# 214 added products of the identity ahead of 43 of TensorE's tasks in a state-space and FFN block

## The chip, the core and the metric

The kernel runs on one core of a Trainium2 chip. The metric is the time of one execution on the device, in microseconds (us); lower is better. A core has five engines that run side by side, each through its own queue, in the order written: TensorE (PE in the profile; its weight loads are PEld), VectorE (DVE), ScalarE (ACT), GpSimd (POOL) and SyncE (SP), which here issues nearly all DMA transfers. TensorE writes only to PSUM, eight banks of 128 partitions by 512 float32 each. The profile also tells the granted clock of TensorE, as a share of full speed.

## What is computed

The reference, cut to what matters. A layer norm modulated by a condition `c`, a long convolution (a diagonal state-space kernel, in the reference through an FFT of 4096 points), and a gated FFN behind a second modulated layer norm. L is 2048, D 640, N 128, FF 1728; all float32.

```python
def _A_ref(u, log_A_real, A_imag, C_real, C_imag, log_dt, D_skip):
    dt = jnp.exp(log_dt)
    A = -jnp.exp(log_A_real) + 1j * A_imag
    C = (C_real + 1j * C_imag) * dt[:, None]
    P = jnp.exp((A * dt[:, None])[:, :, None] * pos[None, None, :])
    K = 2.0 * jnp.einsum("dn,dnl->dl", C, P).real
    y = irfft(rfft(u_t, 2 * L) * rfft(K, 2 * L))[:, :, :L]
    return y + u * D_skip
def _B_ref(x, w1, w3, w2):
    return (_silu(x @ w1) * (x @ w3)) @ w2

sa, ca, ga, sb, cb, gb = split(_silu(c) @ w_mod, 6)
x = x + ga * _A_ref(_layernorm(x) * (1 + ca) + sa, ...)
x = x + gb * _B_ref(_layernorm(x) * (1 + cb) + sb, w1, w3, w2)
```

## The kernel before

**Stages.** The convolution is done in five blocks of 128 channels. For a block `b`, the generator builds the kernel K in eight chunks (tasks `g{b}.{c}`): GpSimd makes phases and magnitudes (`ph`, `z0` to `z2`), ScalarE sines (`s0` to `s4`), VectorE their products (`m0` to `m4`), and TensorE multiplies `xx` by `yy` into the tile `kps` (task `g{b}.{c}.p`, 64 matmul records each); ScalarE and VectorE then move `kps` into `ks` (`r` and `d`). The normed input of the block is made by tasks `h{b}.{i}` in tiles `hn`, `hb` and sent through HBM. A first transform of input and kernel follows (`hh{b}.{i}.m` and `k{b}.{i}.m`, tiles `ps`, 16 records each), copied to `sp` by ScalarE or VectorE (`.e`). The second transform is `w{b}.{i}.f` and `w{b}.{i}.k` (tiles `fh` and `fk`); ScalarE holds `fh` in `hz` (`.h`), VectorE multiplies (`.x0`, `.x1`, `.c`, into `fp`), and `z{b}.{j}.z` transforms back into two `fz` tiles, which go to HBM as `zt` (`v0`, `v1`, `o0`, `o1`).

**Before and behind these.** The condition's row is multiplied with `w_mod` (`mr0` to `mr4` and `mc0` to `mc4`, tile `pm`), the row is spread over the partitions (`pr0` to `pr3`, tile `prow`), and parameters are transposed (`q0.t*`, `q1.t*`, tile `ptp`). Behind block 4 come the last inverse step on the rows (`iy0` to `iy7`, then `iyb0` and `iyb1` on data read back from HBM as `izb`), the second layer norm, its transposes (`tp0.k`, `tp1.k`), and the first FFN products (`pp0.k`, `pp1.k`, tile `gu`; then `dn` into `acc`). After that a hand-ordered FFN runs (tiles `X`, `c`, `acc`), in which nothing is changed.

**Order.** Up to the first FFN products all work is a list of tasks in a planner (`Plan`). Each task has an engine, an assumed duration, predecessors, and the buffers it takes and gives. `Plan.place` puts them into one order by assumed times and ranks (`RANKS`); `Plan.run` then calls the tasks' functions in that order, and `InOrder` chains all instructions of an engine, so that no engine runs its instructions in another order than the plan's. The instructions pass through `InOrder`, so that their profile line is that one helper's (L157) whatever the task; groups are told apart by tile names.

**Banks.** `kps` is one bank, its halves used in turn by even and odd chunks (a chunk's product waits until `r` and `d` of the chunk two before it are done). The tiles with the tag `f` rotate through three banks and the tag `x` has one more; `pbank` deals these four out in turn. `tr` has three banks, which the sines use. A task's first instruction waits for its bank to be released by the readers of the tile before, and for its operands. At `border` these pools close and the FFN's open (five accumulators, `acc0` to `acc4`, and three `gu` banks); `tp*` are put into the accumulators' banks, `iyb*` into `gu`.

**A float32 product** shows in the trace as two matmul records, each with its weight load (32 products of `kps` are 64 records); a transpose is one record. The helper that makes a tile of transposes, as one example of such a task:

```python
def turn(self, ps, tag, bufs, src):
    n = src.shape[1]
    pt = ps.tile([P, 512], F32, name="ptp", tag=tag, bufs=bufs)
    for k in range(n):
        self.turned(pt[:, k * P:k * P + P], src[:, k, :])
```

Of the kernel before, what the change touches and what calls it, by code (L numbers as in the profile page):

```python
# [31 lines left out]
G0 = 17  # L32
SIGN = -2 ** 31
RANKS = """
# [133 lines left out]
class Plan:  # L168
# [101 lines left out]
    def run(self):  # L270

        T = self.tasks
        found = [int(x) for x in RANKS.split()]
        searched = [n for n in T if n not in self.own]
        assert len(found) == len(searched)
        self.order = self.place({n: t[4] for n, t in T.items()} | dict(zip(searched, found)))
        for s, f, e, n in self.order:
            if T[n][2]:
                T[n][2](e)


class K:
# [238 lines left out]
    def param_load(self, T, bs):  # L521
        for nm, src in (("cr", self.c_re), ("ci", self.c_im), ("ai", self.a_im)):
            self.nc.sync.dma_start(T[nm], src.rearrange("(k p) n -> p k n", p=P)[:, bs])

    def turn(self, ps, tag, bufs, src):
        n = src.shape[1]
        pt = ps.tile([P, 512], F32, name="ptp", tag=tag, bufs=bufs)
        for k in range(n):
            self.turned(pt[:, k * P:k * P + P], src[:, k, :])
        return pt[:, :n * P].rearrange("p (b c) -> p b c", b=n)  # L530
# [63 lines left out]
    def gen_chunk(self, d0, tabs, off, E, place):  # L594
# [37 lines left out]
        def product():  # L632
            kps = place()
            for e in range(C // 4):
                for q in range(4):
                    i = e * 4 + q
                    for r in range(2):
                        nc.tensor.matmul(kps[q * 32:(q + 1) * 32, e * 64:(e + 1) * 64], xx[:, r, i, :],
                                         yy[:, r, i, :, :].rearrange("p a b -> p (a b)"),
                                         start=(r == 0), stop=(r == 1), tile_position=(0, 32 * q))  # L640
# [432 lines left out]
    def tail_tasks(self, border, cut):  # L1073
# [109 lines left out]
        def rows(b, rank):  # L1183
            for j in range(4 * b, 4 * b + 4):
                u = j // 2

                def inv(j=j, u=u):
                    py = bank[j] = self.pbank(f"iy{j}")
                    for pr in range(2):
                        self.nc.tensor.matmul(py[pr * 64:pr * 64 + 64, :cut], self.wd[j // 4][:, j % 4, pr, :], z[u][pr][:, j % 2, :],  # L1190
                                              start=True, stop=True, tile_position=(0, pr * 64))
# [23 lines left out]
        def last_inv(b):  # L1215
            py = bank["b"] = self.bank(f"iyb{b}").rearrange("p (j d) -> p j d", j=4)
            for j in range(4):
                for pr in range(2):
                    self.nc.tensor.matmul(py[pr * 64:pr * 64 + 64, j], self.wd[b][:, j, pr, :], z["b", b][:, pr, j], start=True, stop=True, tile_position=(0, pr * 64))
# [16 lines left out]
        def prepare(b, rank):  # L1236
# [15 lines left out]
            for k in range(KT):  # L1252
                r = rank + .1 + .1 * k + b

                def tp(k=k):
                    bank["t", b, k] = self.acc_bank(f"tp{b}{k}", k)
                    self.channels(bank["t", b, k], [xn[b, j] for j in range(4)], k)

# [16 lines left out]
        def plain(b, tiles, p, rank, after):  # L1275
            banks = {}

            def mm(k):
                if k == 0:
                    for m in tiles:  # L1280
                        banks[m] = [self.bank(f"gu{b}{m}{i}") for i in range(2 if m < 13 else 1)]
                x = list(self.x_of(X, b, k))
                for m in tiles:
# [423 lines left out]
    def turn_steps(self, T, where, bs):  # L1707
# [8 lines left out]
        def turn(i):  # L1716
            k, o = (i, 0) if n > 1 else (0, i * P)
            if k not in x:
                x[k] = where()
            for b in range(n):  # L1720
                self.turned(x[k][:, o + b * P:o + b * P + P], T[("fi", "at", "ai", "mx")[i]][:, b, :])
            x["v", i] = x[k][:, o:o + n * P].rearrange("p (b c) -> p b c", b=n)
# [89 lines left out]
    def first_tasks(self, b, m):  # L1812
# [6 lines left out]
        def mm(i):  # L1819
            pk[i] = self.psg.tile([P, 512], F32, name=f"ps{b}{m}{i}", tag="f", bufs=3) if b == 0 else self.pbank(f"ps{b}{m}{i}")  # L1820
            for e in range(4):
                x = self.ks[b][:, 4 * i + e, :] if m else xb[:, :, 4 * i + e]
# [28 lines left out]
    def spectra_tasks(self, b):  # L1851
# [6 lines left out]
        def of(m, i):  # L1858
            ps = bank[m, i] = four(self.pbank(f"f{'hk'[m]}{b}{i}"))
            for q in range(2):  # L1860
# [25 lines left out]
        def inverse(j):  # L1886
            p = prod.pop(j).rearrange("p r q d -> p r (q d)")
            for f in range(2):
                bank["z", j, f] = self.pbank(f"fz{b}{j}{f}")
            for r in range(2):  # L1890
                for f in range(2):
# [108 lines left out]
    def early_tasks(self, e):  # L2000
# [76 lines left out]
        def row(k):  # L2077
            if k == 0:
                pm[0] = self.psx.tile([P, 512], F32, name="pm0", tag="x")
            self.mod_row(pm[0], k)  # L2080
        for k in range(KT):
# [17 lines left out]
        def spread(g):  # L2099
            pr[g] = ps.tile([P, 512], F32, name=f"prow{g}", tag="f", bufs=3)  # L2100
            n = 512 if g < 3 else 384
            nc.tensor.matmul(pr[g][:, :n], bc(self.ident[:, 32 * g], 1, P), mt[0][:, :n], start=True, stop=True)

# [22 lines left out]
        def col(k):  # L2126
            if k == 0:
                pm[1] = self.psx.tile([P, 512], F32, name="pm1", tag="x")
            self.mod_row(pm[1], k, w[k])
        for k in range(KT):  # L2130
# [45 lines left out]
```

## Time and profile before

| | |
|---|---|
| time of three runs, median (lowest to highest) | 970.81 us (970.12 to 972.39) |
| the profiled execution, time on the device | 972.31 us |
| the same execution, first to last instruction (span) | 970.5 us |
| PE, DVE, ACT, POOL busy, share of the span | 89%, 72%, 56%, 35% |
| mean granted clock of TensorE | 0.975 |
| DMA | 127.31 MB, mean 131 GB/s |

The span is 1.8 us shorter than the profiled execution's own time, which is at the upper end of the runs. Up to some 290 us VectorE is busy nine tenths of the time in most stretches and TensorE six to nine; from there on TensorE is busy nearly all the time, apart from a stretch around 380 us between the convolution and the FFN. A matmul record's end is modelled, so that records overlap; the distance from one start to the next is the better price of one. In the rows of the timeline the first number is the start, the second the length of a group of records, the bracket at the end the idle time ahead of it and what ended it.

### The profile page before, as it was taken

Reading aid. Unit: us, or ns where it says so; the run is one execution under the profiler, and the core shown is the slowest. Engines: PE = TensorE matmul, PEld = TensorE weight load, DVE = VectorE, ACT = ScalarE, POOL = GpSimd, SP = SyncE. Lnnn points to the kernel's source line nnn. Section 1 sums busy time; section 2 is a strip of 40 time slices with the busy share of each in tenths; the row PEclk is TensorE's granted clock in tenths of the full one; section 3 lists DMA queues with packets and bytes.
Section 4 is the critical chain, followed back from the end, with each engine's and each line's share of the span. In section 5 each row is a group of like instructions: output and inputs, shape, how many; then the busy total and the mean of one; then the engine's idle time right before and its main releaser. Section 6 shows DMA issues by size and latency. Waiting matters only on the chain.

```text
span 970.5 us, 20551 instructions
## 1 busy us (share of the span) xinstructions
PE 859.9 (89%) x7985; PEld 681.8 (70%) x7985; DVE 702.0 (72%) x1395; ACT 546.4 (56%) x1022; POOL 340.5 (35%) x371
## 2 busy tenths in 40 slices
PE   1464787889899997899999999999999999999997
PEld 1132665767778884677777778888788888888775
DVE  7998899999999968886767677557456464645422
ACT  6877788979888851564434455346444344443412
POOL 1797889879799600002111111000011212120000
PEclk9996999999999999799999999999999999999999
DMA  9955453723425268935434422276342322220374
GB/s 218 275 168 191 111 136 95 177 66 106 111 80 152 74 159 206 241 118 182 122 120 139 122 96 68 82 209 194 112 134 64 102 77 86 82 82 28 108 220 133
DMA packets 110506, 127.31 MB, mean 131 GB/s; under 512 B 10568, under 2 KB 90696, under 8 KB 109128
## 3 DMA queue, kind: packets, MB, share of 16 engines
q1 hardware_dynamic: 109032, 125.21, 45.3%
q8 instruction: 63, 1.03, 0.5%
q10 hardware_dynamic: 1376, 0.79, 0.3%
q14 instruction: 35, 0.29, 0.1%
HBM read 95.82 MB, written 30.15 MB: 130 GB/s over the span
## 4 chain that ended last, share of the span: by engine, by line
PE 70%; DVE 17%; ACT 5%; issue 4%; DMA 3%; POOL 1%; SPq 1%; ACTq 0%; DVEq 0%
PE c L157 19%; PE acc L157 18%; PE X L157 12%; PE ps L157 4%; PE gu L157 3%; DVE yy L157 3%; PE kps L157 3%; PE fz L157 2%; PE fk L157 2%; DVE fp L157 2%; PE fh L157 2%; DVE hn L157 2%; DVE xx L157 2%; DVE xb L157 1%; ACT tr L157 1%
## 5 line engine op out<-in xcount | busy, mean ns | idle before, releaser
L157 PE MATMUL acc<-ah,w 128*128 128x512 f32 x560 | 173.2, 395 | 2.4 <-DMA w<-w2d 1.7
L157 PEld LDWEIGHTS acc<-ah,w 128*128 128x128 f32 x560 | 103.7, 188 | 26.4 <-issue 2.1
L157 PE MATMUL acc<-al,w 128*128 128x512 f32 x260 | 102.4, 394 | 0.0
L665 DVE TENSOR_TENSOR wl<-s,wh 128x256 fp32r<-128x256 f32 x92 | 38.9, 423 | 67.5 <-ACT wh L664 67.1
L841 POOL TENSOR_TENSOR s<-wr 128x256 f32<-128x256 f32 x22 | 16.4, 744 | 187.8 <-DMA wr<-in_w 94.8
L157 POOL TENSOR_TENSOR ph<-p,p 128x1024 int32<-128x1024 int32 x40 | 79.2, 1979 | 8.2 <-ACT tr L157 8.0
L664 ACT ACTIVATE wh<-s 128x256 fp32r<-128x256 f32 x92 | 37.6, 410 | 78.5 <-PE X L157 58.1
L157 PE MATMUL kps<-yy,xx 128*32 128x64 f32 x2560 | 51.8, 234 | 28.6 <-DVE xx L157 21.4
L157 DVE TENSOR_TENSOR yy<-yy,tr 128x512 f32<-128x512 f32 (+1 forms) x80 | 75.3, 943 | 1.2 <-ACT tr L157 0.6
L157 PEld LDWEIGHTS kps<-yy,xx 128*32 128x32 f32 x2560 | 45.1, 116 | 38.3 <-issue 22.0
L664 ACT ACTIVATE wh<-wr 128x256 fp32r<-128x256 f32 x92 | 38.4, 418 | 56.0 <-PE X L157 42.3
L842 POOL TENSOR_TENSOR s<-s,wr 128x256 f32<-128x256 f32 x22 | 16.6, 755 | 134.0 <-issue 133.9
L902 ACT ACTIVATE t<-g 128x512 f32<-128x512 f32 x44 | 27.8, 632 | 52.7 <-DVE g L866 52.7
L157 ACT ACTIVATE tr<-ph,hpi 128x512 f32<-128x512 f32 x80 | 54.6, 690 | 4.4 <-DVE xx L157 2.7
L157 PEld LDWEIGHTS acc<-al,w 128*128 128x128 f32 x260 | 48.9, 188 | 10.8 <-DVE al L665 0.3
L871 DVE SCALAR_TENSOR_TENSOR g<-t,g 128x512 f32<-128x512 f32 x48 | 33.7, 702 | 31.3 <-ACT t L902 29.3
L157 POOL TENSOR_TENSOR yy<-e,e 128x512 f32<-128x512 f32 x48 | 52.4, 1109 | 8.8 <-PE kps L157 5.9
L157 DVE TENSOR_TENSOR xx<-tr,xx 128x512 f32<-128x512 f32 x80 | 54.3, 680 | 1.1 <-ACT tr L157 1.1
L157 PE MATMUL ps<-wk,ks 128*64 128x128 f32 x640 | 42.4, 285 | 13.6 <-DVE ks L157 8.9
L157 ACT ACTIVATE tr<-ph 128x512 f32<-128x512 int32 x80 | 47.3, 598 | 12.4 <-DVE yy L157 6.5
L157 PE MATMUL ps<-wk,xb 128*64 128x128 f32 x640 | 46.1, 295 | 6.3 <-ACT sp L157 3.0
L157 PEld LDWEIGHTS ps<-wk,ks 128*64 128x64 f32 x640 | 37.0, 143 | 20.3 <-ACT hn L157 6.6
(448 smaller groups left out, 2379.7 us busy)
## 6 DMA issues: line engine op xcount, KB each, us to landing
w<-w2d SPq DMA_DIRECT2D x42, 640.0 KB, 3.9
wr<-in_w SPq DMA_DIRECT2D x50, 320.0 KB, 3.9
zd<-zt SPq DMA_DIRECT2D x40, 256.0 KB, 2.9
w2d<-w SPq DMA_DIRECT2D x14, 640.0 KB, 3.5
xs<-in_x SPq DMA_DIRECT2D x16, 320.0 KB, 11.3
hs<-hb SPq DMA_DIRECT2D x20, 256.0 KB, 2.5
xb<-hs SPq DMA_DIRECT2D x20, 256.0 KB, 4.9
iz<-zd SPq DMA_DIRECT2D x32, 160.0 KB, 5.0
```

What stands on the lines that cost most here:

```text
L157: self.prev = self.k.order(f(*a, **kw), self.prev)
L664: self.nc.scalar.activation(H, v, AF.Copy)
L665: eng.tensor_tensor(Lo, v, H.bitcast(F32), op=ALU.subtract)
L841: eng.tensor_tensor(s[0], u[:, 0:2], u[:, 2:4], op=ALU.add)
L842: eng.tensor_tensor(s[1], s[0], g[:, 0:2], op=ALU.subtract)
L871: V.scalar_tensor_tensor(g, th, 1.0, g, op0=ALU.add, op1=ALU.mult)
L902: tanh = lambda o, i: A.activation(o, i, AF.Tanh, scale=0.5)
```

## The change

A planner-wide table `FILL` gives a count for 43 named tasks, 214 in all. While a task is called, its count stands in `plan.fill`; a new function `fill` issues that many products of the 128x128 identity with itself into the first 128 columns of the tile that the task is about to write. Each is a float32 product with `start=True` and `stop=True`, and the task's own products overwrite what it leaves. It is called behind the allocation of the tile and ahead of the task's first instruction, so that the first of these products waits for the bank, and the task's own first instruction for its operands. No other instruction, no order, no buffer and no rank is changed; the assumed durations in the plan do not include the new products.

```diff
+FILL = """
+q0.t2:27 mr0:5 pr2:2 g0.0.p:3 g0.1.p:13 g0.4.p:1 g0.5.p:36 hh0.5.m:1 k0.2.m:2 k0.3.m:2 k0.5.m:8 k0.7.m:4 w0.1.f:9 z0.0.z:3
+w0.2.k:1 w0.5.f:2 g1.2.p:10 g1.3.p:4 k1.0.m:2 k1.1.m:3 k1.6.m:2 w1.3.k:4 g2.0.p:10 g2.1.p:1 g2.3.p:8 g2.4.p:1 k2.2.m:2 w2.2.k:1
+g3.2.p:2 g3.3.p:1 w3.0.k:2 w3.1.f:1 w3.4.k:1 g4.2.p:1 g4.4.p:1 k4.5.m:1 iy3:4 iyb0:6 tp0.0:14 iyb1:7 tp1.1:1 tp1.3:3 tp1.4:2
+"""
...
+        fill = {k: int(v) for k, v in (x.split(":") for x in FILL.split())}
         for s, f, e, n in self.order:
+            self.fill = fill.get(n, 0)
             if T[n][2]:
                 T[n][2](e)
...
+    def fill(self, out):
+        for _ in range(self.plan.fill):
+            self.nc.tensor.matmul(out[:, :P], self.ident, self.ident, start=True, stop=True, skip_group_check=True)
+
     def turn(self, ps, tag, bufs, src):
         n = src.shape[1]
         pt = ps.tile([P, 512], F32, name="ptp", tag=tag, bufs=bufs)
+        self.fill(pt)
...
         def product():
             kps = place()
+            self.fill(kps)
...
                     py = bank[j] = self.pbank(f"iy{j}")
+                    self.fill(py)
...
+            py = self.bank(f"iyb{b}")
+            self.fill(py)
+            py = bank["b"] = py.rearrange("p (j d) -> p j d", j=4)
...
                     bank["t", b, k] = self.acc_bank(f"tp{b}{k}", k)
+                    self.fill(bank["t", b, k])
...
             pk[i] = self.psg.tile([P, 512], F32, name=f"ps{b}{m}{i}", tag="f", bufs=3) if b == 0 else self.pbank(f"ps{b}{m}{i}")
+            self.fill(pk[i])
...
+            ps = self.pbank(f"f{'hk'[m]}{b}{i}")
+            self.fill(ps)
+            ps = bank[m, i] = four(ps)
...
                 bank["z", j, f] = self.pbank(f"fz{b}{j}{f}")
+            self.fill(bank["z", j, 0])
```

The call stands in the same way ahead of the first `pm` row of `mr0` and `mc0`, of `spread` (`pr*`), of the transposes `q*` and of the first FFN products; only tasks that `FILL` names issue anything.

More of the change, by code (lines that the diff above doesn't have):

```diff
@@ L1215, in last_inv @@
         def last_inv(b):
-            py = bank["b"] = self.bank(f"iyb{b}").rearrange("p (j d) -> p j d", j=4)
+            py = self.bank(f"iyb{b}")
+            self.fill(py)
+            py = bank["b"] = py.rearrange("p (j d) -> p j d", j=4)
             for j in range(4):
@@ L1281, in mm @@
                         banks[m] = [self.bank(f"gu{b}{m}{i}") for i in range(2 if m < 13 else 1)]
+                    self.fill(banks[tiles[0]][0])
                 x = list(self.x_of(X, b, k))
@@ L1719, in turn @@
                 x[k] = where()
+            self.fill(x[k][:, o:])
             for b in range(n):
@@ L1858, in of @@
         def of(m, i):
-            ps = bank[m, i] = four(self.pbank(f"f{'hk'[m]}{b}{i}"))
+            ps = self.pbank(f"f{'hk'[m]}{b}{i}")
+            self.fill(ps)
+            ps = bank[m, i] = four(ps)
             for q in range(2):
@@ L2079, in row @@
                 pm[0] = self.psx.tile([P, 512], F32, name="pm0", tag="x")
+                self.fill(pm[0])
             self.mod_row(pm[0], k)
@@ L2101, in spread @@
             n = 512 if g < 3 else 384
+            self.fill(pr[g])
             nc.tensor.matmul(pr[g][:, :n], bc(self.ident[:, 32 * g], 1, P), mt[0][:, :n], start=True, stop=True)
@@ L2128, in col @@
                 pm[1] = self.psx.tile([P, 512], F32, name="pm1", tag="x")
+                self.fill(pm[1])
             self.mod_row(pm[1], k, w[k])
```

## The prediction

> **What bounds the kernel now.** I read the page first.
>
> ```profile
> PE 859.9 (89%) x7985; PEld 681.8 (70%) x7985; DVE 702.0 (72%) x1395; ACT 546.4 (56%) x1022; POOL 340.5 (35%) x371
> DVE  7998899999999968886767677557456464645422
> PEclk9996999999999999799999999999999999999999
> PE 70%; DVE 17%; ACT 5%; issue 4%; DMA 3%; POOL 1%; SPq 1%; ACTq 0%; DVEq 0%
> ```
>
> VectorE is full in the first third, TensorE behind it, and the chain that ended last is 70% TensorE. The added products remove no work; all that they can buy is clock. So the second view is the windows, cut where the stretches at half clock begin and end: these bounds lie 3.41 us apart, or multiples of it.
>
> ```profile
> 78.43:81.84 3.41, 1.15 (x64) 1.02 (x64) 3.37 (x7) 3.09 (x6) 2.94 (x3) 1.00 0.78 296
> 92.09:95.50 3.41, 2.82 (x72) 1.96 (x72) 2.02 (x6) 3.39 (x6) 2.04 (x3) 0.50 0.78 199
> 98.91:102.32 3.41, 1.86 (x24) 1.01 (x24) 3.41 (x7) 1.62 (x3) 3.27 (x5) 1.00 0.33 96
> 102.32:105.73 3.41, 2.42 (x40) 2.01 (x40) 2.81 (x7) 2.81 (x7) 2.90 (x2) 1.00 1.04 210
> 105.73:109.15 3.42, 2.73 (x74) 2.49 (x68) 2.41 (x5) 2.28 (x5) 1.65 (x2) 0.50 0.88 163
> 187.66:191.07 3.41, 1.54 (x24) 1.30 (x26) 3.41 (x6) 3.29 (x5) 3.02 (x8) 1.00 0.39 110
> 208.14:211.55 3.41, 1.38 (x66) 1.32 (x68) 3.41 (x6) 2.88 (x5) 1.79 (x2) 1.00 0.00 0
> 211.55:214.96 3.41, 3.41 (x10) 0.94 (x9) 2.74 (x5) 2.92 (x6) 3.41 (x4) 0.50 0.30 82
> 382.22:385.63 3.41, 0.92 (x12) 0.73 (x14) 3.07 (x12) 0.00 (x0) 0.00 (x0) 1.00 1.00 239
> 392.46:395.87 3.41, 2.59 (x11) 2.25 (x12) 3.31 (x14) 2.72 (x4) 0.00 (x0) 0.50 1.07 219
> 395.87:399.28 3.41, 3.41 (x15) 3.12 (x14) 3.23 (x8) 3.41 (x7) 0.00 (x0) 0.50 1.06 237
> ```
>
> The first number behind the length is TensorE's busy time, the third from the end the granted clock. Stretches with 34%, 45%, 40% and 27% of TensorE (1.15, 1.54, 1.38 and 0.92 of 3.41) are followed by half clock, one with 54% (1.86) is not. Behind one at half clock that is 80% to 100% busy (2.82, 2.73, 3.41) the clock is full again. The one of 2.42 that was followed by half holds eight products of 4 columns. I take half a stretch as the bound.
>
> The third view is the timeline of TensorE, with the idle time that the products are to fill.
>
> ```profile
> 20.82 0.48 PE L157 MATMUL ptp<-ident,late 128*128 128x128 f32 x1 [12.08 <-DVE late L157]
> 46.41 1.96 PE L157 MATMUL kps<-yy,xx 128*32 128x64 f32 x64
> 52.27 1.96 PE L157 MATMUL kps<-yy,xx 128*32 128x64 f32 x64 [2.86 <-POOL xx L157]
> 53.95 1.97 PE L157 MATMUL pm<-wb,sc 128*32 128x512 f32 x8
> 92.68 1.96 PE L157 MATMUL kps<-yy,xx 128*32 128x64 f32 x64 [12.10 <-DVE xx L157]
> 108.09 1.59 PE L157 MATMUL ps<-wk,ks 128*64 128x128 f32 x16 [0.69 <-DVE ks L157]
> 126.63 1.14 PE L157 MATMUL fk<-sp,wb 128*64 128x128 f32 x16
> 128.13 1.15 PE L157 MATMUL kps<-yy,xx 128*32 128x64 f32 x64 [0.36 <-DVE xx L157]
> 130.53 1.13 PE L157 MATMUL fh<-sp,wb 128*64 128x128 f32 x16 [1.25 <-issue]
> 210.17 1.15 PE L157 MATMUL kps<-yy,xx 128*32 128x64 f32 x64 [2.42 <-DVE xx L157]
> 385.12 1.52 PE L157 MATMUL iyb<-izb,late 128*64 128x128 f32 x16 [1.61 <-DMA izb<-zd]
> 387.68 1.94 PE L157 MATMUL iyb<-izb,late 128*64 128x128 f32 x14 [1.04 <-DMA izb<-zd]
> 393.28 4.79 PE L157 MATMUL tp<-ident,xn 128*128 128x128 f32 x20 [3.66 <-ACT xn L157]
> ```
>
> The page tells full clock ahead of 58 us, but the `kps` groups at 46.41 and 52.27 take 1.96 us, as at 92.68 at half clock, against 1.15: TensorE starts at half clock. The large waits sit ahead of q0.t2, g0.5.p and tp0.0. Ahead of w0.1.f (the `fh` group between 124.68 and 126.63) and g0.0.p (46.41), with 9 and 3 products, there is none; ahead of g1.2.p, with 10, there is 0.36 us.
>
> **The price of one product.** It is two passes of 128 columns, each with a 128x128 weight load.
>
> ```profile
> 103.50 1.05 PE L157 MATMUL pv<-ident,mc 128*128 128x4 f32 x8
> 642.69 1.03 PE L157 MATMUL to<-ident,oc 128*128 128x128 f32 x8
> ```
>
> Eight transposes, one such pass each, take 1.03 us with the last one's tail, so about 0.11 a pass; the 20 at 393.28 take 4.79 at half clock, 0.22 a pass. Eight loads of full weights with products of 4 columns take 1.05, 0.13 each. If the load hides behind the pass before, as it does for the transposes, a product costs 0.22 us at full clock and 0.43 at half; if not, 2 x (0.13 + 0.11) = 0.48. No row has this form; I take 0.22, by the transposes. Below 0.21 (two passes) it can't go. Its bank waits are those that the task had already.
>
> **Part by part, up to 58 us (48 products).** From 8.74 (20.82 - 12.08) on, 27 x 0.43 = 11.6 us fit into the 12.08 of q0.t2: nothing. Three at half clock put g0.0.p back by 1.3, so that the 13 start near 50.7 (52.27 - 2.86 + 1.3). If the clock is full from the next bound at about 51.1, they last until 53.8, and `kps`, `pm` and the `ps` group behind them take some 1.05 each instead of 1.9: they end 0.9 sooner. If it rises a stretch later, at 54.5, the 13 end at 55.4 and the three 0.7 later than before. I take 0, between -0.9 and +0.8.
>
> **58 to 124 us (56 products).** The 36 of g0.5.p take 36 x 0.22 = 7.9 of 12.10 us. The remaining 4.2 hold more than half a stretch idle, so the clock is at half again when `kps` starts, as before: 0 (-1.6 if it held: 1.96 less 1.15 for `kps`, and about as much for the `pm` group behind it). Ahead of k0.7.m (108.09, in a stretch at half clock) stand 4 x 0.43 = 1.72 against a wait of 0.69: +1.0, and +0.2 at full clock. The one of hh0.5.m: +0.2. The rest lies in waits.
>
> **124 to 284 us (66 products).** This is where VectorE and ScalarE lead, and where TensorE's lateness counts as far as it exceeds what its readers have to spare.
>
> ```profile
> 130.44 0.36 ACT L157 ACTIVATE ks<-kps 128x256 f32<-128x256 f32 x1
> 131.70 0.60 ACT L157 ACTIVATE hz<-fh 128x512 f32<-128x512 f32 x1 [0.90 <-PE fh L157]
> 134.65 0.60 ACT L157 ACTIVATE tr<-ph 128x512 f32<-128x512 int32 x1 [1.07 <-DVE yy L157]
> 394.70 0.78 ACT L157 ACTIVATE v<-tp,cols 128x512 f32<-128x512 f32 x1 [0.66 <-PE tp L157]
> ```
>
> Nine products at w0.1.f are 2.0 us of lateness, ten at g1.2.p less 0.36 make it 3.8. ScalarE reads that `kps` at 130.44, 1.16 behind its end at 129.28. At 131.70 it waits already now for the `fh` group of 130.53; ahead of that TensorE has 1.25 idle, so the group and with it ScalarE come 2.6 later. Ahead of 134.65 ScalarE has 1.07 idle: 1.5 remain, and VectorE's products wait for that sine. I take +1.5; 0.5 if later idle time takes up the rest, 3.9 if nothing does. On the other side the chain of waits:
>
> ```profile
> 126.66 1.13 PE fk L157 x16
> 163.28 3.51 DMA xq<-in_x
> 211.32 3.46 PE fz L157 x8
> 312.55 1.92 PE fz L157 x8
> 398.07 8.88 PE gu L157 x36
> ```
>
> At 126.66 TensorE is on it, at 163.28 a load: clock bought there is not on the path. At 211.32 `fz` takes 3.46 at half clock, against 1.92 at full. The eight products of g2.3.p (1.8 us in a wait of 2.42) bring the stretch from 208.14 to over 90%: -1.5. Ten at g2.0.p go into the idle time behind it; the other small counts add some +0.9 (0 to 1.5).
>
> **284 to 374 us (7 products).** TensorE never rests.
>
> ```profile
> 330.00:340.00 10.00, 10.00 (x187) 8.44 (x185) 9.00 (x17) 8.51 (x15) 5.03 (x4) 1.00 0.24 69
> ```
>
> Two fit into a wait, five lie on the path: 5 x 0.22 = +1.1 (2.4 by the higher price).
>
> **374 to 412 us (37 products).** Four ahead of iy3 put the rows' steps back by 0.9, hidden behind the DMA for which iyb0 waits until 385.12. Six for iyb0 bring the stretch from 382.22 to (0.92 + 6 x 0.22) / 3.41 = 66%, so that the clock should hold; 7 x 0.22 = 1.5 follow ahead of iyb1, and 14 x 0.22 = 3.1 lie in tp0.0's 3.66. At full clock iyb0 ends 0.6 sooner and the 20 transposes take half of 4.79, so that `gu` could start 3.0 sooner than 398.07; its first four products, at half clock up to 399.28, are 0.8 quicker. But `v` (394.70, 0.78) and the two splits behind it then set its start, where the transposes do now, so I take -2.2, between -3.8 and +0.3 (the clock stays down until the 21 products themselves raise it).
>
> By the Trainium skill, TensorE: Matmul & The Clock Gate, the table "Why this matters for your kernels", only idle gaps over about 3 us bring the clock down; then the eight of g2.3.p buy nothing and the sum is 1.5 higher. The row of 208.14 speaks against it: a wait of 2.42 was enough.
>
> **The sum:** 0 + 1.2 + (1.5 - 1.5 + 0.9) + 1.1 - 2.2 = +1.0 us. The profiled execution took 972.31 us, 1.81 beside its span and 1.50 over the median of the runs; the sum is a difference, so I put it on the median, 970.81: **971.8** (973.3 on the execution's own time). The lower ends, -0.9 - 1.4 - 1.0 + 1.1 - 3.8, make -6.0; the upper, 0.8 + 1.2 + 5.4 + 2.4 + 0.3, make +10.1.
>
> **Rivals.** *The clock holds* (0.27): the long waits stay covered, -1.6 at 92.68, -0.9 at 52, -1.5 at 211, -3.8 behind 382, against 0.4 up to 124, 0.5 at 126, 0.5 for the small ones and 1.1 behind 284: -5.3, so 965.5. For it: the greatest counts stand ahead of the longest waits. Against it: 7.9 us don't fill 12.10, and an idle 4.2 is more than the 2.42 that was enough at 210.17.
>
> *The loads don't hide* (0.14), which ends slower: a product takes 0.48 us. Then g0.5.p ends 36 x 0.48 - 12.10 = 5.2 late, tp0.0 14 x 0.48 - 3.66 = 3.1, the 19 at 126 cost 4.9 more, the five behind 284 1.3 more: 1.0 + 14.5, so 986. It decides from 12.10 / 36 = 0.34 us a product on. The transposes, 0.11 a pass with a load of the same size, stand against it.
>
> *The transposes let the clock fall* (0.14): behind tp0 one more stretch is at half, and `gu` loses 1.7 there: 973.5. The rows from 392.46 on bear it out in part: 76% (2.59 of 3.41), nearly all transposes, did not raise the clock, 80% of products at 105.73 did. It is also the rule of Part 4, PE-mode transpose, of the page named above, in the Trainium skill: transposes don't count as activity.
>
> That the products don't fall into the waits at all is excluded where a bank is free early, as that of `kps` is; it is the lateness counted above where it isn't.
>
> **How the numbers follow.** My forecast, no change to a little slower, has the remaining 0.45 and 969 to 976 as its own range. A measurement of this kernel tells 0.2% (1.9 us) from no change. Of the forecast 0.08 go to faster, 0.20 to the same and 0.17 to slower; of the first rival 0.25 to faster and 0.02 to the same; of the second all to slower; of the third 0.04 to the same and 0.10 to slower: 0.33, 0.26 and 0.41. The range, 965 to 980, leaves out the dear product and the best of all clocks.
>
> **What would show it.** In the profile of the changed kernel the 36 products ahead of g0.5.p should last about 8 us, then some 4 idle, and the `kps` group behind them 1.96. The first `fz` group behind g2.3.p should take 1.92, the 20 transposes of tp0 half of 4.79, and ScalarE's copy of `fh` behind g1.2.p should wait some 2.6 longer. I am wrong if products are more than 0.3 us apart, if the clock is at half still when tp0 starts, if TensorE's stretch behind 284 us is no longer than before, or if the windows show other stretches at half clock than this.

## The result, and the profile after

| kernel | median of its runs, us | from, to, us | span of the profiled execution, us |
|---|---|---|---|
| before | 970.96 | 970.12 to 972.39 | 970.5 |
| changed | 979.73 | 977.80 to 980.84 | 976.0 |

The ratio is 1.0087, with a 95% interval from 1.0066 to 1.0107: the change makes the kernel 8.8 us slower. The forecast was 971.8 within 965 to 980; the sign was the likeliest of the three. The range held only just, 0.3 us inside its end, and the forecast's own range of 969 to 976 was missed: the sum of +1.0 us was much too small. The profiled execution of the changed kernel (977.8 us) is the shortest of its four runs, that of before (972.31) is near the top of its runs, so the two spans are only 5.5 us apart.

The head of the page of the changed kernel, and the shares of its chain of waits:

```profile
PE 905.0 (93%) x8413; PEld 725.8 (74%) x8413; DVE 702.4 (72%) x1395; ACT 546.2 (56%) x1022; POOL 340.7 (35%) x371
...
PE 75%; DVE 14%; issue 3%; ACT 3%; DMA 2%; POOL 1%; SPq 1%; DVEq 0%; ACTq 0%
```

The 214 products are 428 passes (8413 - 7985), TensorE is busy 45 us longer (905.0 less 859.9), VectorE as long as before, and TensorE's part of the chain rises from 70% to 75%. The products did buy clock. These are windows of the changed kernel: first the end of the wait of g0.5.p, which its products don't fill, and the stretch behind it; then a place that nothing fills; then the stretch of the tail in which the 20 transposes stand. As in the prediction, the first number behind the length is TensorE's busy time and the third from the end the granted clock.

```profile
89.30:92.71 3.41, 0.46 (x31) 0.49 (x35) 3.41 (x5) 2.83 (x3) 0.85 (x2) 1.00 0.07 21
92.71:96.12 3.41, 3.41 (x86) 2.17 (x80) 1.54 (x4) 3.38 (x6) 3.10 (x5) 0.50 1.00 310
167.81:171.22 3.41, 1.28 (x6) 0.37 (x3) 3.30 (x7) 2.17 (x5) 3.33 (x4) 1.00 0.29 77
171.22:174.63 3.41, 3.17 (x30) 3.17 (x32) 3.27 (x7) 2.35 (x5) 2.72 (x3) 0.50 0.40 112
...
399.91:403.32 3.41, 2.56 (x21) 2.24 (x20) 3.30 (x14) 2.96 (x5) 0.00 (x0) 1.00 1.10 236
```

The rule read from the profile of before holds again: 13% (0.46) and 38% (1.28) busy are followed by half clock, and the tail, at half clock before from 385.63 to 399.28, is at full clock. What came out of that on TensorE, from its timeline:

```profile
80.75 8.30 PE L162 MATMUL kps<-ident 128*128 128x128 f32 x72 [0.63 <-ACT ks L162]
92.25 1.55 PE L162 MATMUL kps<-yy,xx 128*32 128x64 f32 x62 [3.20 <-DVE xx L162]
...
211.24 2.05 PE L162 MATMUL kps<-ident 128*128 128x128 f32 x16
213.76 1.16 PE L162 MATMUL kps<-yy,xx 128*32 128x64 f32 x64 [0.47 <-DVE xx L162]
214.85 1.99 PE L162 MATMUL fz<-fp,wz 64*128 64x512 f32 x8
...
400.65 0.50 PE L162 MATMUL tp<-ident,xn 128*128 128x128 f32 x2 [0.66 <-ACT xn L162]
401.34 2.20 PE L162 MATMUL tp<-ident,xn 128*128 128x128 f32 x18 [0.20 <-DVE xn L162]
...
404.67 0.50 PE L162 MATMUL gu<-x0l,wh_u 128*128 128x512 f32 x1 [0.85 <-DVE x0l L162]
```

Most of what the prediction said would show it is there: the 36 products last 8.30 us, then 3.20 us are idle and `kps` falls into half clock; `fz` behind g2.3.p takes 1.99, where before it took 3.53 (3.46 on its chain); the 20 transposes take 2.7 instead of 4.79, and `gu` then waits 0.85 us for VectorE's split. So where does the time go? Four instructions that both kernels have, as marks, first before:

```profile
59.75 1.17 PE L157 MATMUL kps<-yy,xx 128*32 128x64 f32 x64
122.62 1.17 PE L157 MATMUL kps<-yy,xx 128*32 128x64 f32 x64
288.84 1.99 PE L157 MATMUL fz<-fp,wz 64*128 64x512 f32 x8
373.19 1.99 PE L157 MATMUL fz<-fp,wz 64*128 64x512 f32 x8 [1.17 <-DVE fp L157]
```

The same four in the changed kernel:

```profile
58.74 1.17 PE L162 MATMUL kps<-yy,xx 128*32 128x64 f32 x64
122.53 1.17 PE L162 MATMUL kps<-yy,xx 128*32 128x64 f32 x64
293.31 1.99 PE L162 MATMUL fz<-fp,wz 64*128 64x512 f32 x8
380.74 1.99 PE L162 MATMUL fz<-fp,wz 64*128 64x512 f32 x8 [1.17 <-DVE fp L162]
```

And in the changed kernel profiled a second time (e8_again, below):

```profile
60.06 1.17 PE L162 MATMUL kps<-yy,xx 128*32 128x64 f32 x64
124.79 1.17 PE L162 MATMUL kps<-yy,xx 128*32 128x64 f32 x64
294.37 1.99 PE L162 MATMUL fz<-fp,wz 64*128 64x512 f32 x8
381.95 1.99 PE L162 MATMUL fz<-fp,wz 64*128 64x512 f32 x8 [1.17 <-DVE fp L162]
```

The differences of each mark, less that of the mark ahead, give the stages; the last row takes the spans (970.5, 976.0 and 977.4). The last column is the kernel before, profiled a second time (e11_before_again, below): its marks stand at 59.28, 123.53, 289.55 and 374.72, its span is 971.3.

| from mark to mark (times of before) | forecast, us | changed | changed, again | before, again |
|---|---|---|---|---|
| start to 59.75 | 0 | -1.0 | +0.3 | -0.5 |
| to 122.62 | +1.2 | +0.9 | +1.9 | +1.4 |
| to 288.84 | +0.9 | +4.6 | +3.4 | -0.2 |
| to 373.19 | +1.1 | +3.1 | +3.2 | +0.8 |
| to the end | -2.2 | -2.0 | -1.9 | -0.7 |

In the first two stages and in the last the forecast is near the traces. But two executions of the same kernel differ by up to 1.4 us in a stage, and three kernels of the experiments that have no product ahead of 284 us (e2, e3 and e4) are 1.5 to 2.8 us later than before in the third stage of their traces. So a stage of one trace proves little, for or against. The loss lies between 122 and 373 us, where many tasks were given one to four products each; it has to be followed task by task. Here is such a place in the changed kernel, w3.4.k, with the tasks on either side:

```profile
321.62 1.08 PE L162 MATMUL fh<-sp,wb 128*64 128x128 f32 x16
322.63 0.49 PE L162 MATMUL fk<-ident 128*128 128x128 f32 x2
323.05 1.14 PE L162 MATMUL fk<-sp,wb 128*64 128x128 f32 x16
324.02 1.08 PE L162 MATMUL fh<-sp,wb 128*64 128x128 f32 x16
```

The `fh` groups of the same place before:

```profile
315.37 1.08 PE L157 MATMUL fh<-sp,wb 128*64 128x128 f32 x16
...
317.19 1.08 PE L157 MATMUL fh<-sp,wb 128*64 128x128 f32 x16
```

From `fh` to the next `fh` it is 1.82 us before and 2.40 after (324.02 - 321.62): a single product costs 0.58 us there, not 0.22. The figure behind the operation is the part of the array in use: 128*64 for the `fh` and `fk` groups, 128*128 for the product. The suspicion that the experiments test: not the product is dear, but leaving the column tiles for full width and coming back.

### The profile page after: what moved, and what is told of

The parts are those of the page before. It is cut to its first block, busy times and chain, and to the rows that moved or that the text cites. A ratio compares the mean times of both kernels' runs of the same rounds, so it can differ in the third digit from the quotient of the medians.

```text
span 976.0 us, 21401 instructions
## 1 busy us (share of the span) xinstructions
PE 905.0 (93%) x8413; PEld 725.8 (74%) x8413; DVE 702.4 (72%) x1395; ACT 546.2 (56%) x1022; POOL 340.7 (35%) x371
## 3 DMA queue, kind: packets, MB, share of 16 engines
q8 instruction: 66, 1.08, 0.5%
## 4 chain that ended last, share of the span: by engine, by line
PE 75%; DVE 14%; issue 3%; ACT 3%; DMA 2%; POOL 1%; SPq 1%; DVEq 0%; ACTq 0%
PE c L162 19%; PE acc L162 18%; PE X L162 12%; PE ps L162 7%; PE kps L162 4%; PE gu L162 3%; PE fk L162 3%; PE fh L162 3%; PE fz L162 3%; DVE yy L162 2%; PE iy L162 2%; DVE xb L162 1%; DVE fp L162 1%; DVE hn L162 1%; DVE xx L162 1%
## 5 line engine op out<-in xcount | busy, mean ns | idle before, releaser
L162 PE MATMUL kps<-yy,xx 128*32 128x64 f32 x2560 | 49.4, 229 | 11.3 <-DVE xx L162 9.0
L162 PEld LDWEIGHTS kps<-yy,xx 128*32 128x32 f32 x2560 | 43.0, 113 | 20.0 <-issue 12.5
L162 PEld LDWEIGHTS ps<-wk,xb 128*64 128x64 f32 x640 | 44.1, 220 | 11.5 <-ACT zt L162 3.2
L678 DVE TENSOR_TENSOR wl<-wr,wh 128x256 fp32r<-128x256 f32 x92 | 40.4, 440 | 14.9 <-ACT wh L677 14.8
```

The source lines that it names most:

```text
L162: self.prev = self.k.order(f(*a, **kw), self.prev)
L678: eng.tensor_tensor(Lo, v, H.bitcast(F32), op=ALU.subtract)
```

## The experiments

Each was timed in five rounds beside the kernel before, on the same chip; the difference is the ratio less 1 times that session's median of before (973.17 for the first four, 973.33, 974.62 and 972.59 for the later ones). All lists are lists of `FILL`.

**One product a task, or seven.** Both kernels have 28 products and no others.

```diff
-q0.t2:27 mr0:5 pr2:2 ... tp1.3:3 tp1.4:2
+hh3.3.m:1 hh3.7.m:1 k3.0.m:1 k3.1.m:1 ... w4.3.k:1 w4.4.k:1    (e2_singles: 28 tasks)
+k3.0.m:7 w3.2.f:7 hh4.0.m:7 k4.4.m:7                            (e3_blocks)
```

> No other products than 28, one each in 28 of the hh, k and w tasks between 284 and 366 us, where TensorE never rests. Theory (0.22 us and about 0.3 once for each task): 28 x 0.53 = 14.8, so about 985.8 us. Rival (a product costs 0.22 wherever it stands, and the stage behind 284 us was longer by another cause): 28 x 0.226 = 6.3, so 977.3. The profile should show each one with a gap of some 0.18 us ahead of its weight load and another behind it.

> The same 28 products in four blocks of seven (k3.0, w3.2.f, hh4.0, k4.4). Theory: 28 x 0.226 + 4 x 0.3 = 7.5, so 978.5 us, seven below the singles. Rival (0.5 us is the price of a product, not of a task): 28 x 0.53 = 14.8, 985.8 as for the singles. Second rival (no price of the task): 6.3, 977.3, and the singles the same.

Measured: singles 1.0134 (1.0113 to 1.0155), +13.0 us; blocks 1.0093 (1.0076 to 1.0111), +9.1 us. The singles are dear as expected and dearer than the same products in blocks, but by 4.0 us and not by 7. Two tasks of the singles, each with its product, on TensorE:

```profile
321.05 0.49 PE L160 MATMUL fh<-ident 128*128 128x128 f32 x2
321.47 1.14 PE L160 MATMUL fh<-sp,wb 128*64 128x128 f32 x16
...
323.45 0.49 PE L160 MATMUL fh<-ident 128*128 128x128 f32 x2
```

And in the blocks, one block, and the place where that kernel lost something else:

```profile
309.60 1.35 PE L160 MATMUL fk<-sp,wb 128*64 128x128 f32 x10 [1.68 <-issue]
...
337.45 1.83 PE L160 MATMUL ps<-ident 128*128 128x128 f32 x14
339.21 3.29 PE L160 MATMUL ps<-wk,xb 128*64 128x128 f32 x48
```

A period with one product takes 2.40 us, 0.58 more than the 1.82 of before. The block of seven holds TensorE for 1.76 us (339.21 - 337.45), 0.25 a product. So most of the price is one of the task. The blocks' total is larger than 7.5. In the profiled execution, a middling one of the six, a wait for instructions of 1.68 us stands in the way (0.56 before), behind which the clock was at half for a stretch (309.84 to 313.26); whether the other runs had the same is not known.

**The same singles in column tiles.**

```diff
-            self.nc.tensor.matmul(out[:, :P], self.ident, self.ident, ...)
+            for f in range(2):
+                self.nc.tensor.matmul(out[f * 64:f * 64 + 64, :P], self.ident[:, f * 64:f * 64 + 64], self.ident, ..., tile_position=(0, 64 * f))
```

> The 28 singles, each issued as two products of 64 columns side by side, in the column tiles that the task's own products use: the same number of sums. Theory (the price of the task comes from changing between full width and column tiles): none is left, 28 x 4 passes x 0.067 us (16 passes of a w task take 1.08) = 7.5, so 978.5 us. Rival (it comes from breaking the stream, by the bank or by what each task begins with): 7.5 + 28 x 0.3 = 15.9, so 986.9.

Measured: 1.0062 (1.0044 to 1.0079), +6.0 us, less than half of the singles at full width. Two tasks again:

```profile
319.44 0.39 PE L160 MATMUL fh<-ident 128*64 128x128 f32 x4
...
321.48 0.39 PE L160 MATMUL fh<-ident 128*64 128x128 f32 x4
```

The period is 2.04 us, 0.22 more than before. With the same sums in the tiles of its neighbours, the product costs what the forecast took; at full width it costs 0.58. The difference, 0.36 us, is the price of the change of shape there and back. The theory holds, and the rival (that any foreign product breaks the stream) falls. A second rival is that the tiles are cheaper since their weight loads are half as wide. The single records speak against it: around the product of e2_singles at 321.05, the last pass of one shape and the first of the next start 0.20 us apart on both sides (320.85 and 321.05, 321.27 and 321.47), and no load begins between them. In before, from an `fh` group to a `kps` group, the distance is 0.20 as well (318.00 and 318.20), though the loads behind it are narrower there (32 columns instead of 64).

**Only waits, or only small counts.** Two kernels that split the change by whether TensorE waits there.

```diff
+q0.t2:27 mr0:5 g0.1.p:13 g0.5.p:36 k0.5.m:8 g2.0.p:10 g2.3.p:8 iyb0:6 tp0.0:14 iyb1:7         (e1_waits)
+k1.6.m:2 w1.3.k:4 g2.1.p:1 g2.4.p:1 k2.2.m:2 w2.2.k:1 g3.2.p:2 g3.3.p:1 w3.0.k:2 w3.1.f:1 w3.4.k:1 g4.2.p:1 g4.4.p:1 k4.5.m:1 iy3:4   (e12_small)
```

> 134 of the 214 products, only in tasks that have a wait to put them in: q0.t2 27, mr0 5, g0.1.p 13, g0.5.p 36, k0.5.m 8, g2.0.p 10, g2.3.p 8, iyb0 6, tp0.0 14, iyb1 7. Theory (a product costs 0.22 us, but a task without a wait that is given one or two costs some 0.3 us more, once, for leaving the column tiles and coming back): the small counts carried the loss, so this kernel keeps the clock and loses nothing, about 966.5 us, that is 970.96 less 0.9 ahead of 58 us, 1.3 at fz behind g2.3.p and 2.8 at the tail, with 0.5 of the clock gained early lost again. Rival (the long fills themselves cost the time, by the clock or by the loads of the same time): at or above 971.

> Only the small counts behind 165 us, at full width: 27 products in 15 tasks (k1.6.m 2, w1.3.k 4, g2.1.p, g2.4.p, w2.2.k, g3.3.p, w3.1.f, w3.4.k, g4.2.p, g4.4.p and k4.5.m 1 each, k2.2.m, g3.2.p and w3.0.k 2 each, iy3 4). Theory (each product 0.226 us, each task that TensorE has no wait for 0.25 to 0.33 more): in the trace of the changed kernel taken again twelve of these tasks put TensorE back by 0.2 to 1.24 us, 7.5 in all, so about +7.5 us, ratio 1.0077. Rival (the forecast's price, 0.22 a product, with iy3 hidden and those up to 284 us partly): at most +2.5 us, ratio 1.0025.

Measured: the waits alone 0.9979 (0.9964 to 0.9993), -2.0 us; the small counts alone 1.0053 (1.0033 to 1.0073), +5.2 us. So these 25 products (the 27 of the expectation is a miscount) carry most of the loss, though less than the 7.5 expected, and the 134 in waits win a little, half of what I expected. The trace of e1_waits shows where a part of the rest went: its wait for instructions at 305.65 us lasts 2.21 us, and in the tail the six products of iyb0 left the stretch from 384.64 at 48% busy, so that the next one was at half clock. One of its tasks, g2.0.p, has no wait ahead of it (its ten products put TensorE back by 2.43 us, which later idle time took up). The small counts, one by one: the four products of w1.3.k between an `fh` group and its `fk` group (e12_small).

```profile
197.66 1.08 PE L160 MATMUL fh<-sp,wb 128*64 128x128 f32 x16
198.67 1.16 PE L160 MATMUL fk<-ident 128*128 128x128 f32 x8
199.76 1.13 PE L160 MATMUL fk<-sp,wb 128*64 128x128 f32 x16
```

Set against before in order, this task is put back by 1.24 us, as iy3 with four is; k2.2.m with two by 0.79, w3.4.k and k4.5.m with one by 0.57. That is 0.226 a product and 0.34 once. The `kps` tasks g2.4.p and g4.4.p with one lose 0.42, g3.2.p with two 0.64: 0.226 a product and 0.19 once (g2.1.p, 0.57, does not fit). Ahead of a `kps` group the shape changes anyway, from 128*64 to 128*32; the product adds one change there and two elsewhere, so each change costs some 0.17 to 0.19 us. The Trainium skill, TensorEngine Tiling (Array Packing), section Tiling Modes, Key Properties, has the rule, "Mode switching requires drain", without a price; these runs agree with it and give one.

**All 214 in tiles, and the change once more.**

```diff
-    def fill(self, out):
+    def fill(self, out, n=P):
         for _ in range(self.plan.fill):
-            self.nc.tensor.matmul(out[:, :P], self.ident, self.ident, ...)
+            for c in range(0, P, n):
+                self.nc.tensor.matmul(out[c:c + n, :P], self.ident[:, c:c + n], self.ident, ..., tile_position=(0, c))
...
-            self.fill(kps)
+            self.fill(kps, 32)
...
-            self.fill(pk[i])
+            self.fill(pk[i], 64)
```

> All 214 products as in the change, but in the column tiles that the task's own products use: two of 64 columns in the hh, k, w and iy tasks, four of 32 columns in the kps tasks; full width as before in the transposes, the rows and z0.0.z. Theory (some 0.3 us a task for changing to full width and back): about a dozen tasks on the path lose it, so 3.6 us less than the change: about +5 on before, ratio 1.0055. Rival (that price is a small part of the loss): ratio 1.008 to 1.010, as the change. Second rival (products in tiles keep the clock up less, as they use a part of the array at a time): kps behind g0.5.p and fz behind g2.3.p at half clock, and the time above the change's.

> The changed kernel once more, unaltered, timed on the same chip as its parts. Theory (the wait of 2.00 us for TensorE's instructions at 311 us depends on when the load of the block happens to land, and is no part of the change): its length differs by more than 0.5 us from 2.00 in this execution, and the ratio to before is 1.009 again. Rival (it belongs to this program): 2.0 us at the same instruction.

Measured on one chip: in tiles 1.0028 (1.0012 to 1.0043), a median of 975.81; the change itself 1.0066 (1.0042 to 1.0089), 979.28. The 3.5 us between them are the 3.6 of the theory; both ratios are lower than I had put them (1.0055 and 1.009). Between the two traces the distance grows along the way, 1.5 us at 160 us, 2.6 at 289, 3.2 at 380 (times of before), as a price of many tasks would. The clock is kept up as well by tiles: behind g2.3.p `fz` again takes 1.99.

```profile
215.12 1.99 PE L162 MATMUL fz<-fp,wz 64*128 64x512 f32 x8
```

**The stage from 124 to 165 us.**

```diff
+w0.1.f:9 z0.0.z:3 w0.2.k:1 w0.5.f:2 g1.2.p:10 g1.3.p:4 k1.0.m:2 k1.1.m:3     (e5_stage124: only these)
...
-w0.1.f:9 z0.0.z:3 w0.2.k:1 w0.5.f:2 g1.2.p:10 g1.3.p:4 k1.0.m:2 k1.1.m:3     (e9_without124: all but these)
```

> Only the 34 products between 124 and 165 us: w0.1.f 9, z0.0.z 3, w0.2.k 1, w0.5.f 2, g1.2.p 10, g1.3.p 4, k1.0.m 2, k1.1.m 3. Theory (the lateness of w0.1.f and g1.2.p is not taken up by later idle time, and the small ones cost their 0.3 each): the trace of the change shows 2.8 us more at 160 us than at 124, of which a part may be absorbed by the load at 163; so +1.5 to +2.8, 972.5 to 973.8 on the median of before. Rival (VectorE and ScalarE take the lateness up by 200 us): no difference, 970 to 972.

> The change without the 34 products between 124 and 165 us (w0.1.f, z0.0.z, w0.2.k, w0.5.f, g1.2.p, g1.3.p, k1.0.m, k1.1.m), all others as they were. Theory (their lateness stays): 2 to 2.8 us less than the changed kernel, a ratio to before of about 1.0045. Rival (later idle time takes it up, and all of the loss comes from the small counts behind it): ratio 1.0065, as the changed kernel on the same chip.

Measured: alone 1.0015 (0.9995 to 1.0035), which is -0.5 to +3.4 us and holds both the theory and the rival; the change without them 1.0069 (1.0042 to 1.0095), no less than the change (1.0066, on another chip), though the theory's 1.0045 is just inside. So what these products cost stays open. Without them these are windows of e9_without124, in the slowest of its six runs:

```profile
166.60:170.00 3.40, 3.13 (x68) 2.48 (x70) 3.18 (x9) 1.88 (x5) 2.32 (x5) 0.50 0.29 80
170.00:173.43 3.43, 1.35 (x6) 0.28 (x4) 3.36 (x6) 2.79 (x6) 3.35 (x5) 1.00 0.46 129
173.43:180.25 6.82, 5.99 (x72) 5.66 (x76) 6.60 (x14) 3.16 (x5) 3.07 (x3) 0.50 0.76 210
```

Three stretches at half clock stand here that the change has only one of (171.22), and none in its second profile. From 122 to 160 us TensorE falls back by 3.7 us in both traces of the change and by 0.1 here; from 160 to 180 us it loses 3.6 here, where the change gains 0.4 and 1.5. In these traces the products save about as much of clock as they cost in lateness; that this is so in every execution is not shown.

**The tail and g2.3.p alone, and a version that gains.**

```diff
+g2.3.p:8 iyb0:6 tp0.0:14 iyb1:7                                                         (e6_tail, full width)
+q0.t2:27 mr0:5 g0.1.p:13 g0.5.p:50 k0.5.m:8 g2.3.p:8 iyb0:6 tp0.0:14 iyb1:7             (e10_waits_tiled, with the tiles of e7)
```

> Only g2.3.p 8, iyb0 6, tp0.0 14 and iyb1 7, 35 products that all stand in waits. Theory (the clock that they buy is gained whole): 1.3 at fz behind g2.3.p and 2 to 2.8 at the tail, so 3.3 to 4.1 us less than before, ratio 0.996. Rival (the clock needs the earlier products too, or other waits, as those for TensorE's next block of instructions, give it back): less than 1.5 us gained.

> 138 products, only ahead of tasks with waits, in the column tiles of their tasks: q0.t2 27, mr0 5, g0.1.p 13, g0.5.p 50 instead of 36, k0.5.m 8, g2.3.p 8, iyb0 6, tp0.0 14, iyb1 7. Theory (nothing of it is late, and 50 products, 11.2 us, keep the clock through the wait ahead of g0.5.p): kps behind g0.5.p takes 1.15 us instead of 1.96, fz behind g2.3.p 1.92 to 1.99, and the kernel is 3 us faster than before, ratio 0.997. Rival (a part of the gain is lost to other waits, for instructions or for VectorE): ratio 0.998 to 1.000, as for the same waits at full width.

Measured: e6_tail 0.9997 (0.9978 to 1.0017), not told from before, although its profiled execution, the fastest of the twelve, has a span of 966.4. Its twelve runs go from 968.18 to 977.48, those of before from 969.55 to 977.94: the gain of 3.3 us that I expected isn't shown. e10_waits_tiled 0.9959 (0.9935 to 0.9983), -4.0 us, with a median of 970.56 beside 974.62: faster than before and, by the ratios, than the change. Its wait ahead of g0.5.p, with 50 products:

```profile
81.51 11.14 PE L160 MATMUL kps<-ident 128*32 128x128 f32 x400 [0.63 <-ACT ks L160]
93.09 1.10 PE L160 MATMUL kps<-yy,xx 128*32 128x64 f32 x62 [0.44 <-DVE xx L160]
...
304.80 0.48 PE L160 MATMUL fh<-sp,wb 128*64 128x128 f32 x2 [3.65 <-issue]
```

The clock holds, and `kps` takes 1.10 where the change needed 1.55 and before 1.96. But in e1_waits, with 36 products and the same 3.20 us idle, it held too: the bounds of the stretches fell so that the two which share the idle time, from 87.69 and from 91.10, were 58% and 48% busy; in e10_waits_tiled none there is under 87%.

```profile
92.89 1.10 PE L160 MATMUL kps<-yy,xx 128*32 128x64 f32 x62 [3.20 <-DVE xx L160]
```

So what the 14 more bring is that it no longer depends on where the bounds fall. How much of the 4.0 us is due to the tiles, to the 50, or to leaving out g2.0.p was not tried one by one. The row at 304.80 is what it doesn't avoid.

**The kernel before, again.**

> The kernel before, unaltered, for a second profile. Theory (the wait for TensorE's next block of instructions between 300 and 312 us is in every one of these kernels, 0.56 to 2.6 us long, and its length is a matter of the execution): it differs from 0.56 us here by more than 0.3. Rival (the added instructions make it longer): 0.56 again. By the spread of the runs of before on this chip, the ratio is 1.000 within 0.002.

Measured: 0.9994 (0.9977 to 1.0011). The wait for instructions at 306 us is 1.12 us instead of 0.56, so it moves by 0.56 without any change; but in the changed kernel it was 2.00 and 1.73, which differ by less than the 0.5 that I had expected there. Whether more instructions make it longer stays open.

## Why the prediction was right or wrong

**The price of a product, 0.22 us, was right as far as it went.** In a block, 72 passes take 8.30 us, 0.113 each with the last one's tail taken off. But the rows that it came from, the transposes, stand among instructions of their own shape, and no row of before had a full-width product between column tiles. That was said ("No row has this form"), and bounded by a price of the load, 0.48 a product; what was missing is a price per task, 0.34 us, or 0.19 ahead of `kps`. The rival that a product costs 0.48 everywhere is wrong: the 36 did fit into their wait.

**Up to 122 us** 0 and +1.2 were forecast, -1.0 and +0.9 measured in the first profile, +0.3 and +1.9 in the second. No step is refuted, but the sums prove little: before's own second trace has -0.5 and +1.4. Of the -1.0, 0.9 is there already at 20.82 us, where VectorE made `late` 0.9 sooner. The 27 products of q0.t2 last 7.3 and 7.9 us and not 11.6, as a part of them ran at full clock. Task by task, g0.0.p was put back by 1.3 and k0.7.m by 0.8 and 0.9, as forecast; hh0.5.m, with one product, by 0.5 and 0.8 instead of 0.2.

**124 to 284 us is the step that failed**, and in it the term "the other small counts add some +0.9 (0 to 1.5)". It is for 29 products. Seventeen of them stand ahead of 195 us; with the nine, the ten of g1.2.p and the ten of g2.0.p they put TensorE back by 11 us in passing, and at 198 us 1.0 of it is left in the first profile (0.7 in the second): there later idle time, and clock gained by the way, do take up nearly all. Behind 195 us they don't: in the first profile g2.1.p puts TensorE back by 0.57, w1.3.k by 1.24, g2.4.p by 0.42, k2.2.m by 0.79, g3.2.p by 0.64, w2.2.k by 0.42 and g3.3.p by 0.20: 4.3 us, for 12 products. At 0.22 these would be 2.6 already, so two things were wrong: the price of the task, and that idle time would take up most of it here as well. Once TensorE sets the pace, what it loses stays lost, as the shift that stands still from 268 to 300 us shows. The +1.5 for w0.1.f and g1.2.p lies above what is left there, 1.0 for all of these together, but within its 0.5 to 3.9. The -1.5 for g2.3.p was 1.99 - 3.53 = -1.54, but against this execution of before. The row of before, then that of before profiled again, where no product stands either:

```profile
211.25 3.53 PE L157 MATMUL fz<-fp,wz 64*128 64x512 f32 x8
```

```profile
213.27 1.99 PE L157 MATMUL fz<-fp,wz 64*128 64x512 f32 x8
```

Of the seven traces without these eight products six have a stretch at half clock there, of the seven with them none. So the products do hold the clock, and what they are worth differs by execution.

ScalarE's copy of `fh` came 2.8 us later, as forecast (2.6), but its wait is no longer (0.68, before 0.90): ScalarE waits 1.54 for the copy of `kps` just before it:

```profile
133.45 0.38 ACT L162 ACTIVATE ks<-kps 128x256 f32<-128x256 f32 x1 [1.54 <-PE kps L162]
134.51 0.60 ACT L162 ACTIVATE hz<-fh 128x512 f32<-128x512 f32 x1 [0.68 <-PE fh L162]
```

**284 to 374 us:** +1.1 forecast, 3.1 measured. w3.1.f and g4.4.p lose 0.42 each, w3.4.k and k4.5.m 0.57 each, 2.0 in all; w3.0.k is hidden, as forecast; g4.2.p, which was counted, loses 0.42 too, but 0.40 of it is made up again before w3.4.k. The rest is a wait for TensorE's own instructions, 2.00 us after and 0.56 before, which the prediction hadn't seen, and which differs between executions. The row after, and then the row before:

```profile
311.48 0.52 PE L162 MATMUL kps<-yy,xx 128*32 128x64 f32 x18 [2.00 <-issue]
```

```profile
304.99 1.15 PE L157 MATMUL kps<-yy,xx 128*32 128x64 f32 x61 [0.56 <-issue]
```

**The tail:** -2.2 forecast, -2.0 and -1.9 measured, to the end of the program. Up to 430 us (time of before) it is -1.5 in both; the rest comes behind 910 us, where nothing was changed and where every other trace, that of before taken again too, is ahead of the first one of before. The four products of iy3 were costed at nothing, as hidden behind a DMA. They put TensorE back by 1.24 us, and the wait for that DMA does take it up (0.81 us of the wait are left in the first profile, 0.32 in the second); but VectorE, which reads `iy` and then works without a break from 386.74 on, starts later too. The two kernels with the tail's products but without iy3's gain 2.0 (e10_waits_tiled) and 2.4 (e6_tail) up to 430 us, so by these four traces iy3 cost 0.5 to 0.9, and the clock gave about what was taken for it. It is the clock that changed: in the seven traces without the tail's products three or four stretches are at half there, in the seven with them none, but for one in e1_waits, which gained 0.5. That the sum came out so near is in part luck: e2 and e3, without a product there, gain 1.5 and 1.7 up to 430 us, as one stretch less at half clock falls into it in their executions than in the first of before.

**Of the rivals**, "the clock holds" (965.5) was right about the tail and g2.3.p and wrong at 92.71, where the change left 3.20 us idle; there it is a matter of the bounds, as e1_waits shows. "The transposes let the clock fall" is refuted in this kernel: the stretch from 399.91 in the change is 75% busy, with hardly anything but the 20 transposes, and full clock follows. In before, profiled again, a stretch at half clock holds nothing but transposes, and full clock follows:

```profile
394.94:398.35 3.41, 3.40 (x17) 3.29 (x17) 3.18 (x16) 2.72 (x5) 0.00 (x0) 0.50 0.97 211
```

The 76% at 392.46 that didn't raise the clock are no sign of transposes: in e9_without124 the stretch from 173.43 is as busy (2.58 of 3.41), with products of `ps`, and didn't raise it either. On the Trainium skill's rule of idle gaps over about 3 us, weighed in the prediction (TensorE: Matmul & The Clock Gate, "Why this matters for your kernels"), the eight products of g2.3.p decided for the rows: they fill a wait of 2.42 us, and the clock holds behind it in each of the seven traces that have them. Of the signs of being wrong two came: a product costs over 0.3 us in the small counts, and a stretch at half clock stands at 171.22 that wasn't foreseen.

**What isn't settled** is the whole of the 8.8 us. The marks account for 5.5 us in one profile and 6.9 in another, and the ratio of the second session is +6.4 us. The parts, each on another chip, make +4.7 (-2.0, +5.2 and +1.5), without the 21 products that no part has. The runs of before spread over 8.4 us on that chip (969.55 to 977.94), at mean granted clocks from 0.956 to 0.977, those of the change by 3.5 us (977.92 to 981.44), at 0.975 to 0.983. So in these runs the change's clock is the steadier one as well (six runs against 29), and how much it loses depends on which runs of before it is set against.

## What to carry to other kernels

Work that is to keep an engine's clock up must have the shape of its neighbours, the same part of the array, and belongs only ahead of waits that the trace shows, in a number that nearly fills them, so that it doesn't matter where the clock's stretches begin; one product in a stream that never rests costs as much as two and a half in a block. A price taken from a row holds for that row's surroundings: ask what stands ahead of it and behind it there. And where a kernel's runs differ by more than the effect, set the stages of several profiles against each other before a sum is believed.

## What the runs showed of the hardware

- **A change of shape has a price.** Going from 128*64 to 128*128 and back costs 0.34 to 0.36 us at full clock, with one change less 0.19. At each change the first pass starts 0.20 us behind the last one of the other shape, and no weight load begins in between, whether the next loads are wider or narrower. Among full-width products a pass takes 0.113 us, its load included.
- **How busy a stretch has to be.** Cut into the clock's stretches of 3.41 us, from 58 us on, the fourteen traces agree. At full clock, a stretch under 40% busy is always followed by half clock, one over 54% never, but for the one around 103 us that holds the eight products of 4 columns (64% to 71%); in between both occur. At half clock, full clock follows from about 80% on.
- **TensorE waits for its instructions, always at the same place of a block.** The page counts the loads, 16 KB each (1.08 MB in 66). With TensorE's instructions counted in the trace, the waits for nothing but issue, behind 200 us, stand at number 6338 and 8386 before, 7106 and 9155 in the change, 9667 in e10_waits_tiled: all leave 194 or 195 when divided by 256. The counts of the loads fit 256 instructions each: 63 loads for 16144 instructions of TensorE in before, 66 for 16994 in the change, 69 for 17631 in e10_waits_tiled, 71 for 18358 in e7_all_tiled. One stands between 300 and 315 us in every trace here, whichever block is due then, and one between 248 and 262 in most; they last from 0.44 to 3.65 us.

```profile
q8 instruction: 66, 1.08, 0.5%
```

- **The phase of the clock's stretches is not that of the program.** The first stretch that the trace marks at half clock begins at 21.03 us in one execution of the changed kernel and at 18.85 in the other. The first trace of before marks none ahead of 58 us, though its `kps` groups at 46.41 and 52.27 took 1.96; the change's marks 23.9 us there. So the mean clocks of the two are not counted alike.
